# Float64 weights converted on four engines: Pool's integer sum moved from before the final merge to after it, in place on the weights

## The chip, the cores and the metric

The program runs on one core of one Trainium2 chip. A core has five engines, each with its own in-order queue of instructions: TensorE (PE, matrix products, with weight loads shown as PEld), VectorE (DVE), ScalarE (ACT), GpSimd (Pool) and SyncE (SP, which issues the transfers). [...]The metric is the device time of one execution in microseconds (us); lower is better.

## What is computed

The reference is a routed attention block followed by a feed-forward block:

```python
q_assign = argmax(q_n @ c_n.T);  k_assign = argmax(k_n @ c_n.T)        # 16 clusters per head
scores   = where(q_assign == k_assign, q @ k.T / sqrt(64), -1e9)       # batch 4, 8 heads, 768 tokens, 64 wide
attn_out = softmax(scores) @ v
x = attn_out as (3072, 512)
h = x @ w_in                                                          # w_in (512, 2048)
sp = log(1 + exp(h));  g = h * erf(sp)
out = (g @ w_out).astype(float32)                                     # w_out (2048, 512)
```

q, k, v and the centroids come as float32. The two weight matrices come as float64, so on the chip each value is two 32-bit words: a high word (sign, 11 bits of exponent, 20 of fraction) and a low word (the last 32 bits of the fraction). [...]the kernel makes float32 from the two words by integer operations.

## The kernel before

**Attention.** Heads go two at a time: 16 pairs (4 batches of 4 pairs), each with two halves of the queries (384 columns) and 6 blocks of 128 keys, which makes 12 units a pair. For a pair, `route` (line 276) transposes q and k on VectorE and finds clusters, and `shift` (line 352) computes bf16 products `sm` on TensorE, takes their row maxima `nmx` on VectorE, folds these into `nm`, transposes `nm` on TensorE (`pn`), copies it on ScalarE (`nmT`) and sends it by small transfers into a row of `qm`. For a unit, `scores` (line 409) makes `sc` on TensorE and exponentiates it into `pr` on ScalarE; `accumulate` (427) sums `pr` into `acc` on Pool; `attend` (440) multiplies `pr` by v into `av`. After 6 units `divide` (452) sums `acc` on TensorE (`psum`), makes its reciprocal with ScalarE's Ln and Exp (`inv`), refines it on VectorE (`den`) and writes the scaled `av` into `xT`.

**Feed-forward.** The 3072 tokens are 12 chunks of 256. `hidden` (line 519) multiplies `w_in` by `xT` into `hp`, which VectorE copies to `g`; `gate` (497) makes softplus and erf in two tiles `a_s` on ScalarE and multiplies them into `g` on Pool; `project` (543) multiplies `g` by `w_out` into `po`. These products are yielded one by one by `ffn_stream` (562) and fed between the attention units by `pump` (586). `sm`, `psum`, `pn`, `psim`, `hp`, `po` and `av` share one pool of four PSUM buffers, `sc` has two of its own. Softplus, erf, Ln and Exp lie in different function tables of ScalarE, and a table load goes in front of each that finds another table active.

**Conversion.** There are 32 steps (`w_steps`, line 172), each a block of 128 x 512 weights: 16 of `w_in`, then 16 of `w_out`. `fetch` (188) starts a step's transfer of 512 KB. The block lands in a quarter of the `w_out` tile that is not in use yet (places 0 to 3, so the trace calls these staging blocks `w_out`), or, for the late steps, in one of the two `a_s` tiles of the gate (place 4). The quarter also holds two scratch blocks: `m` for the rounding bits and `x` for the shifted value. One step is then

1. ScalarE: `x = |high word|` and `m` from the low word (`split`, 200);
2. VectorE: `x = max(x, tiny)`;
3. VectorE: `x = x << 3`, which puts exponent and fraction where float32 has them;
4. Pool: `x = x + m`, an integer sum that adds the three last bits, rounded, and mends the exponent's bias;
5. VectorE: `weights = (high word & sign bit) | x` (`join`, 207).

`convert` (215) is a generator with three yields a step. In its third part of step n it joins step n-1 (not n), starts a transfer, and splits step n+1. So the join of a step stands in VectorE's queue behind the maximum and shift of the next step. `converted` counts joined steps, and `hidden` and `project` yield nothing useful while a block that they need is not counted.

**Order.** `prepare(n)` (594) takes n parts of `convert`. Up to slot 44 of 48 (the first batch's units) the order in each queue is that of the program: the tuple `plan` (606) says for each of a pair's 12 slots how many parts of routing and of conversion go in front. From slot 45 (`FIRST`) on, `in_order` is off and a list scheduler with its own estimates places the instructions; `prepare(2)` is then called in each of five places per pair of units (line 702), except for some rest after a gate.

Of the kernel before, what the change touches and what calls it, by code (L numbers as in the profile page):

```python
# [8 lines left out]
F32 = mybir.dt.float32  # L9
BF16 = mybir.dt.bfloat16  # L10
U32 = mybir.dt.uint32
I32 = mybir.dt.int32
ALU = mybir.AluOpType
ACT = mybir.ActivationFunctionType
# [3 lines left out]
P = 128  # L18
# [48 lines left out]
def kernel(  # L67
# [13 lines left out]
    te, ve, ae, ge = (  # L81
        InOrder(tc, e, in_order) for e in (nc.tensor, nc.vector, nc.scalar, nc.gpsimd)
    )

    def pool(name, bufs, **kw):
        return ctx.enter_context(tc.tile_pool(name=name, bufs=bufs, **kw))

    const = pool("const", 1)
# [78 lines left out]

    two = const.tile([P, 1], F32, name="two")  # L170
    ve.memset(two, 2.0)
    w_steps = []
    for c in range(0, DFF, LC):
        for r in range(DM // P):
# [1 line left out]
    n_w_in = len(w_steps)  # L176
# [4 lines left out]
    converted = [0]  # L181

    def half_tile():
        return actp.tile([P, NFT // 2, TB], F32, name="a_s")

    steps = {}

    def fetch(done):

        for n in range(max(done + 1, 0), min(done + 5, len(w_steps))):  # L190
            at = places[n]
            if n in steps or (at < 4 and at in places[done + 1 : n]) or (at == 4 and n > done + 2):
                continue
            t = half_tile() if at == 4 else w_out[:, 4 * at : 4 * (at + 1)]
            t = t.rearrange("p f t -> p (f t)").bitcast(U32)
            nc.sync.dma_start(out=t[:, 0 : 2 * LC], in_=w_steps[n][1])
            raw = t[:, 0 : 2 * LC].rearrange("p (n w) -> p n w", w=2)
            steps[n] = raw[:, :, 1], raw[:, :, 0], t[:, 2 * LC : 3 * LC], t[:, 3 * LC : 4 * LC]

    def split(n):  # L200

        if n < len(w_steps):
            hi, lo, m, x = steps[n]
            ae.activation(out=x.bitcast(F32), in_=hi.bitcast(F32), func=ACT.Abs)
            ae.activation(out=m.bitcast(F32), in_=lo, func=ACT.Identity, bias=two, scale=2.0**-51)

    def join(n):
        hi, _, _, x = steps[n]
        ve.scalar_tensor_tensor(
            out=w_steps[n][0].bitcast(U32), in0=hi, scalar=0x80000000, in1=x,  # L210
            op0=ALU.bitwise_and, op1=ALU.bitwise_or,
        )
        converted[0] = n + 1

    def convert():

        split(0)
        for n in range(len(w_steps)):
            _, _, m, x = steps[n]
            xf, xi = x.bitcast(F32), x.bitcast(I32)  # L220
            ve.tensor_scalar(out=xf, in0=xf, scalar1=TINY_HI, scalar2=None, op0=ALU.max)
            yield
            ve.tensor_scalar(out=x, in0=x, scalar1=3, scalar2=None, op0=ALU.logical_shift_left)

            ge.tensor_tensor(out=xi, in0=xi, in1=m.bitcast(I32), op=ALU.add)
            yield
            if n > 0:
                join(n - 1)

                fetch(n - 2 if n < n_w_in else n - 1)  # L230
            split(n + 1)
            yield
        join(len(w_steps) - 1)

    load_qk(0)
    fetch(-1)
# [17 lines left out]
    for it in range(2):  # L254
# [4 lines left out]
            out=twice, in0=ss, scalar=inv, in1=norm, op0=ALU.mult, op1=ALU.add  # L259
# [3 lines left out]
            out=norm, in0=twice, scalar1=0.5, scalar2=(1e-6 if it else 0.0),  # L263
            op0=ALU.mult, op1=ALU.add,
# [325 lines left out]


    conv = convert()

    def prepare(n):
# [26 lines left out]
    for e in range(2):  # L621
        ve.tensor_copy(
            out=ccT[e * D : (e + 1) * D, :, e * C : (e + 1) * C],
            in_=pct[e * D : (e + 1) * D].rearrange("d (r e c) -> d r e c", e=2, c=C)[:, :, e],
# [10 lines left out]
    for e in range(2):  # L635
        ve.reduce_sum(
            out=own[:, e : e + 1],
            in_=ident.rearrange("p (g x c) -> p x g c", x=2, c=C)[:, e], axis=AX.XY,
# [106 lines left out]
```

## Time and profile before

The median is 1236.87 us over three runs (1235.66 to 1238.39). The profiled execution spans 1232.8 us.

| engine | busy us | share of the span |
|---|---|---|
| PE | 1162.9 | 94% |
| ACT | 568.8 | 46% |
| DVE | 534.6 | 43% |
| POOL | 464.9 | 38% |

The shares are averages over unlike stages. The first conversion instruction on ScalarE starts at 20.3 us and the last join ends at 285.6 us, so conversion touches only the first 290 us; the rest is attention and feed-forward products without a pause. In what follows, a line of the profile reads: source line (nearly always L58, the helper through which all operations are recorded, so that tiles tell them apart), engine, operation, tile written <- tiles read, shapes, count, then busy time, mean ns of one, and the idle time in front of them with what ended it. In a timeline the two first numbers are start and length in us.

The conversion's own instructions, from the groups of the trace by shape: ScalarE's absolute value takes 672 ns and its rounding 755 ns; VectorE's maximum and shift take 587 and 578 ns in the mean in the `w_out` places (median 427 for the two together), its join 866 to 958 ns in the mean (median 684 to 693); Pool's sum 1397 ns in the mean (median 1275).

### The profile page before, as it was taken

How to read it: one execution, taken by the hardware profiler on the slowest of the kernel's cores; microseconds unless marked ns; L12 is line 12 of the kernel's file. 1: busy time of each engine (PE TensorE's matmuls, PEld its weight loads, DVE VectorE, ACT ScalarE, POOL GpSimd, SP SyncE). 2: the span in 40 equal slices, each digit the busy share in tenths (PEclk: the TensorE clock that was granted, in tenths of full speed). 3: DMA queues.
4: the chain of work that ended last, by engine and by line, in shares of the span. 5: the costliest groups of instructions: out<-in, count | busy, mean ns of one | idle time of the engine just before them, and what ended most of it. 6: DMA issues, size and time to landing. Idle time of an engine off the chain costs nothing.

```text
span 1232.8 us, 13370 instructions
## 1 busy us (share of the span) xinstructions
PE 1162.9 (94%) x4897; PEld 622.3 (50%) x4897; DVE 534.6 (43%) x1000; ACT 568.8 (46%) x674; POOL 464.9 (38%) x462
## 2 busy tenths in 40 slices
PE   4788879988999998999999999999999999999998
PEld 1222236555454455555456455556456456576663
DVE  6888875564534344334344344333335112011121
ACT  3666646548352648165265445346264254032222
POOL 2567754345433344344143244225244343030200
PEclk7999889788999999999999999999999999999999
DMA  7334333131020202011020201002010000000000
GB/s 133 73 90 107 95 85 91 31 103 26 22 47 10 39 9 39 9 24 24 10 47 1 48 9 27 21 10 39 1 31 1 9 9 1 9 9 17 1 18 18
DMA packets 140753, 42.95 MB, mean 35 GB/s; under 512 B 133520, under 2 KB 133520, under 8 KB 140688
## 3 DMA queue, kind: packets, MB, share of 16 engines
q1 hardware_dynamic: 137552, 41.70, 15.2%
q10 hardware_dynamic: 3136, 0.39, 0.3%
q8 instruction: 39, 0.64, 0.2%
q14 instruction: 26, 0.21, 0.1%
HBM read 35.68 MB, written 6.29 MB: 34 GB/s over the span
## 4 chain that ended last, share of the span: by engine, by line
PE 69%; issue 6%; ACT 2%; DVE 2%; POOL 1%; DMA 1%; SPq 0%; ACTq 0%; DVEq 0%
PE po L58 25%; PE hp L58 23%; PE sc L58 10%; PE av L58 6%; PE sm L58 3%; PE psum L58 1%; ACT L58 1%; PE psim L58 1%; ACT inv L58 1%; DVE den L58 1%; POOL a_s L58 0%; DMA a_s<-in_moe_w_out_dram 0%; PE pn L58 0%; DVE w_out L58 0%; DVE xT L58 0%
## 5 line engine op out<-in xcount | busy, mean ns | idle before, releaser
L58 PE MATMUL hp<-xT,w_in 128*128 128x256 f32 x1536 | 387.4, 389 | 7.2 <-DVE xT L58 4.5
L58 PE MATMUL po<-w_out,g 128*128 128x512 f32 x768 | 367.8, 597 | 0.6 <-DVE den L58 0.6
L58 POOL TENSOR_TENSOR acc<-acc,pr 128x384 f32<-128x384 f32 x256 | 240.1, 968 | 321.7 <-ACT pr L58 321.6
L58 PEld LDWEIGHTS hp<-xT,w_in 128*128 128x128 f32 x1536 | 289.8, 193 | 125.1 <-issue 80.9
L58 DVE TENSOR_REDUCE nmx<-sm 128x1 f32<-128x384 f32 x384 | 195.2, 550 | 139.2 <-PE sm L58 138.3
L58 ACT ACT_TABLE_LOAD x112 | 143.7, 1283 | 235.9 <-DVE g L58 131.2
L58 ACT ACTIVATE pr<-sc 128x768 f32<-128x768 f32 x192 | 147.0, 806 | 156.8 <-PE sc L58 154.4
L58 PEld LDWEIGHTS po<-w_out,g 128*128 128x128 f32 x768 | 141.8, 190 | 106.1 <-issue 93.5
L58 PE MATMUL sc<-qT,kT 64*128 64x384 f32 x768 | 189.6, 543 | 4.5 <-ACT pr L58 4.4
L58 POOL TENSOR_TENSOR g<-a_s,g 128x512 f32<-128x512 f32 x88 | 111.1, 1296 | 209.3 <-ACT a_s L58 209.3
L58 DVE COPY g<-hp 128x512 f32<-128x512 f32 x96 | 65.9, 687 | 264.0 <-PE hp L58 263.8
L58 PE MATMUL av<-pr,in_v 128*64 128x386 f32 x768 | 142.9, 502 | 2.2 <-DVE nmx L58 2.2
L58 PE MATMUL sm<-km,qm 128*128 128x384 bf16 x384 | 104.3, 339 | 26.4 <-DVE nmx L58 14.6
L58 PEld LDWEIGHTS sc<-qT,kT 64*128 64x128 f32 x768 | 72.3, 193 | 88.6 <-issue 45.1
L58 POOL TENSOR_TENSOR acc<-pr,pr 128x384 f32<-128x384 f32 x64 | 64.9, 1034 | 102.0 <-ACT pr L58 102.0
L58 PEld LDWEIGHTS av<-pr,in_v 128*64 128x64 f32 x768 | 49.8, 138 | 89.9 <-issue 74.8
L58 PEld LDWEIGHTS <-qm 128*128 128x128 bf16 x384 | 35.1, 99 | 94.4 <-issue 71.8
L58 DVE SCALAR_TENSOR_TENSOR den<-psum,inv 128x384 f32<-128x384 f32 x32 | 17.8, 557 | 144.9 <-ACT inv L58 144.5
L58 PE MATMUL sc<-qm,km 64*128 64x384 bf16 x384 | 60.5, 330 | 2.1 <-DMA qm<-nmT 2.1
L58 ACT ACTIVATE a_s<-g 128x2048 f32<-128x2048 f32 x24 | 45.8, 1910 | 30.8 <-DVE g L58 30.7
L58 ACT ACTIVATE a_s<-a_s 128x2048 f32<-128x2048 f32 (+1 forms) x32 | 51.3, 1602 | 15.1 <-DMA a_s<-in_moe_w_out_dram 14.8
L58 ACT COPY nmT<-pn 6x128 bf16<-6x128 bf16 x32 | 8.0, 251 | 102.8 <-PE pn L58 102.2
(68 smaller groups left out, 609.8 us busy)
## 6 DMA issues: line engine op xcount, KB each, us to landing
w_out<-in_moe_w_in_dram SPq DMA_DIRECT2D x16, 512.0 KB, 4.7
in_q<-in_q_dram SPq DMA_DIRECT2D x64, 96.0 KB, 3.1
in_v<-in_v_dram SPq DMA_DIRECT2D x32, 192.0 KB, 3.0
out_dram<-osb SPq DMA_DIRECT2D x24, 256.0 KB, 2.0
in_k<-in_k_dram SPq DMA_DIRECT2D x60, 96.0 KB, 3.4
a_s<-in_moe_w_out_dram SPq DMA_DIRECT2D x8, 512.0 KB, 3.5
w_out<-in_moe_w_out_dram SPq DMA_DIRECT2D x8, 512.0 KB, 3.4
qm<-nmT SPq DMA_DIRECT2D x192, 0.2 KB, 1.7
```

Source lines behind the costliest of these rows:

```text
L58: ins = getattr(self.engine, name)(*args, **kw)
```

## The change

The conversion's last two operations change places. The shift gets a second operation, which masks the result to its lower 30 bits; the join follows on the same engine, takes the two upper bits of the high word instead of one, and writes the weights; and Pool adds the rounding bits last, in place on the weights. The bias of the exponent, which came in through the constant 2.0 in `m`, is now mended by the mask, so `m` becomes a plain rounded integer and the constant tile `two` goes. The three VectorE operations of a step no longer have Pool's sum between them, and a step is finished within its own turn: there is no join of an earlier step and no join after the loop. The call of `fetch` moves one part forward.

```diff
-    two = const.tile([P, 1], F32, name="two")
-    ve.memset(two, 2.0)
...
             ae.activation(out=x.bitcast(F32), in_=hi.bitcast(F32), func=ACT.Abs)
-            ae.activation(out=m.bitcast(F32), in_=lo, func=ACT.Identity, bias=two, scale=2.0**-51)
-
-    def join(n):
-        hi, _, _, x = steps[n]
-        ve.scalar_tensor_tensor(
-            out=w_steps[n][0].bitcast(U32), in0=hi, scalar=0x80000000, in1=x,
-            op0=ALU.bitwise_and, op1=ALU.bitwise_or,
-        )
-        converted[0] = n + 1
+            ae.activation(out=m.bitcast(I32), in_=lo, func=ACT.Copy, scale=2.0**-29)
...
         for n in range(len(w_steps)):
-            _, _, m, x = steps[n]
-            xf, xi = x.bitcast(F32), x.bitcast(I32)
+            hi, _, m, x = steps[n]
+            w = w_steps[n][0]
+            xf = x.bitcast(F32)
             ve.tensor_scalar(out=xf, in0=xf, scalar1=TINY_HI, scalar2=None, op0=ALU.max)
             yield
-            ve.tensor_scalar(out=x, in0=x, scalar1=3, scalar2=None, op0=ALU.logical_shift_left)
-
-            ge.tensor_tensor(out=xi, in0=xi, in1=m.bitcast(I32), op=ALU.add)
+            ve.tensor_scalar(
+                out=x, in0=x, scalar1=3, scalar2=0x3FFFFFFF,
+                op0=ALU.logical_shift_left, op1=ALU.bitwise_and,
+            )
+
+            fetch(n - 2 if n < n_w_in else n - 1)
             yield
-            if n > 0:
-                join(n - 1)
-
-                fetch(n - 2 if n < n_w_in else n - 1)
+            ve.scalar_tensor_tensor(
+                out=w.bitcast(U32), in0=hi, scalar=0xC0000000, in1=x,
+                op0=ALU.bitwise_and, op1=ALU.bitwise_or,
+            )
+
+            ge.tensor_tensor(out=w.bitcast(I32), in0=w.bitcast(I32), in1=m.bitcast(I32), op=ALU.add)
+            converted[0] = n + 1
             split(n + 1)
             yield
-        join(len(w_steps) - 1)
```

## The prediction, made before the result was known

> **What bounds the kernel now.** I read the page first (busy shares, then slices), then busy time by stretches, because an average can't say which stage the change touches.
>
> ```profile
> 20.00:140.00 120.00, 99.96 (x496) 31.50 (x495) 102.44 (x196) 74.04 (x115) 75.44 (x71) 0.92 0.35 83
> 140.00:200.00 60.00, 48.50 (x205) 23.83 (x205) 47.26 (x76) 28.90 (x45) 35.65 (x32) 0.86 0.35 90
> 200.00:300.00 100.00, 87.35 (x372) 54.05 (x370) 53.53 (x95) 62.27 (x70) 46.57 (x42) 0.86 0.27 62
> 300.00:1233.00 933.00, 920.85 (x3809) 510.91 (x3807) 320.40 (x582) 394.56 (x434) 300.54 (x296) 1.00 0.09 18
> ```
>
> Columns: stretch, its length, busy us of PE, PEld, DVE, ACT, POOL (with counts), PE's granted clock, the share of the DMA engines, GB/s. From 300 us on PE is busy 920.85 of 933 us at full clock. So the kernel is bound by PE, and every us that PE loses before 300 us arrives at the end, while what other engines gain is worth nothing unless PE waited for them. In the three stretches of conversion PE loses 20.0 + 11.5 + 12.7 = 44 us, and its clock is below 1. Until 140 us VectorE is busy 102.44 of 120 us and feeds PE late; afterwards it is not full, so what matters there is what its queue is blocked by. The waits of VectorE over the whole span:
>
> ```profile
> DVE w_out L58 <- POOL a_s L58: 9.2, 6, 3.2
> DVE w_out L58 <- POOL w_out L58: 5.0, 4, 1.5
> DVE w_in L58 <- POOL w_out L58: 1.7, 2, 1.4
> ```
>
> All three are a join that stands at the head of VectorE's queue until Pool's sum is done: 15.9 us, of which only 1.7 lie in the part ordered by the program. The timelines show what stands behind. VectorE, then PE:
>
> ```profile
> 161.87 0.42 DVE L58 TENSOR_SCALAR w_out<-w_out 128x512 uint32<-128x512 uint32 x1
> 163.66 1.47 DVE L58 SCALAR_TENSOR_TENSOR w_in<-w_out 128x512 uint32<-128x512 uint32 x1 [1.38 <-POOL w_out L58]
> 165.06 1.94 DVE L58 TENSOR_REDUCE nmx<-sm 128x1 f32<-128x384 f32 x4
> ...
> 175.32 1.74 DVE L58 SCALAR_TENSOR_TENSOR w_out<-w_out 128x512 uint32<-128x512 uint32 x1 [0.70 <-POOL w_out L58]
> 176.98 1.35 DVE L58 SCALAR_TENSOR_TENSOR den<-den,inv 128x384 f32<-128x384 f32 x1
> 178.25 1.35 DVE L58 SCALAR_TENSOR_TENSOR w_out<-w_out 128x512 uint32<-128x512 uint32 x1
> 179.53 0.74 DVE L58 SCALAR_TENSOR_TENSOR xT<-av,den 128x256 f32<-128x256 f32 x2
> ```
>
> ```profile
> 165.65 0.32 PE L58 MATMUL sm<-km,qm 128*128 128x384 bf16 x1 [2.32 <-DVE nmx L58]
> 168.18 0.27 PE L58 MATMUL pn<-identb,nm 128*6 128x128 bf16 x1 [1.41 <-DVE nm L58]
> 168.38 1.65 PE L58 MATMUL sc<-qT,kT 64*128 64x384 f32 x4
> 172.20 0.92 PE L58 MATMUL sc<-qT,kT 64*128 64x384 f32 x4
> 180.06 8.28 PE L58 MATMUL hp<-xT,w_in 128*128 128x256 f32 x26 [4.48 <-DVE xT L58]
> ```
>
> The join at 163.66 waits 1.38 us, and takes 1.47 instead of 0.68 since Pool's next sum has started; four row maxima stand behind it and PE loses 2.32. The same pattern delays `nm` (PE loses 1.41) and `xT` (4.48). Later, in the same PE timeline, PE waits 1.36 for `nmx` at 248.03, 3.50 for `nm` at 254.46, 1.95 for a `g` copy at 282.69 and 1.95 for `nm` at 285.77; in VectorE's queue the last three stand behind joins that waited 3.19, 1.98 and 0.51 us for Pool.
>
> **What the Trainium skill says.** "SBUF — State Buffer", section "Who interferes with whom": VectorE and GpSimd share a port pair as an exclusive lock, which a VectorE operation takes when it reads two SBUF inputs or runs in a two-port mode (the maximum and shift can, `nmx` from PSUM can't), and the second to come waits fully. The trace agrees: joins take 0.67 to 0.69 us free and up to 1.76 us, the row maxima 0.54 to 0.56 us under the same Pool load. "VectorE: DVE Perf Modes", section "The perf-mode tier table": `tensor_scalar` on fp32 in SBUF runs at two elements a cycle; the shift's free 0.42 us against the join's 0.68 fits. It names no other price for a second operation, and no row of this trace has one at this size. "TensorE: Matmul & The Clock Gate", Part 1: an idle PE falls back to a halved clock. The trace agrees: four `sc` products take 1.65 us just after those stalls and 0.92 later.
>
> **The change, part by part.** Per step there remain two ScalarE operations, three on VectorE and one sum on Pool, of the same sizes. The constant's memset (59 ns) goes; nobody waits for it.
>
> *ScalarE's rounding* loses its bias tile: between 0.67 us (the absolute value's row) and 0.755 us (today's), 32 x 0.08 = 2.7 us at most, hidden behind PE. I count 0. The order of the changed program, though, puts two more table loads into ScalarE's queue near the first gate (one more in the whole program): one exponential now stands between a softplus and an erf, and one absolute value between the next pair. A load is 1.283 us in the trace; at 240 us that delays the second erf and its successors by 1.28 + 0.67 = 1.95 us.
>
> *The shift's mask*: 0.42 us if the second operation is free; at one element a cycle about the join's 0.68, 32 x 0.26 = 8.3 us on VectorE. I take free.
>
> *Shift and join in sequence*: independent neighbours on VectorE overlap by about 0.09 us, dependent ones have a gap of 0.03 to 0.04, so some 0.12 us more, 16 x 0.12 = 1.9 us in the ordered part. About half of it meets PE: minus 1.0.
>
> *Join without Pool's wait, ordered part up to 180 us.* (a) Before `nm`: by the new order one join less lies between the shift at 161.87 and `nm`. From the shift's end, 162.29: four row maxima 1.94, a maximum 0.42 to 1.13, `nm` 0.16, so `nm` ends at 164.8 to 165.5 instead of 168.13. I take 2.9 us. (b) From `nm` to `xT` took 168.13 to 180.27 = 12.1 us, with ten conversion operations between; 5.7 us of it is waits and stretched lengths. In the new order six are left. The sum of free lengths is 2 x 0.68 + 4 x 0.42 + 0.54 + 0.56 + 0.74 = 4.9, but `den` needs `inv`, ready 4.8 us after `nm`, so at least 4.8 + 1.84 = 6.6; with up to 3 us of lock about 8. PE comes for `xT` 7.4 us after `nm`, so its wait falls from 4.48 to about 1: 3.5 us. (c) Clock: after the three stalls PE spends about 1.2 us too much at 168 to 171 and 8.28 - 26 x 0.224 = 2.5 at `hp` (0.224 is 7.17 us over the 32 at 192.56). Of 3.7 I take 1.5.
>
> *The moved operations* (three more after `xT`) land in 180 to 200 us, where VectorE waited for Pool 1.45 us three times: 0.
>
> *Last stage, 245 to 287 us.* Gone: the stalls at 282.69 and 285.77, up to 3.9 us, I take 2.0, since a `g` copy still stands behind conversions. Not gone: at 254.46 `nm` now stands behind the maximum of the next step, which needs a transfer into `a_s`; in the old trace its absolute value starts at 252.11, after a 4.67 us wait for that transfer, and the later erf pushes it. The maximum at 246.83 waited 2.19 us for ScalarE and is pushed too. Minus 2.0. Sum 0.
>
> *Pool's sum last*: the new wait is Pool's, for the join. Behind it in Pool's queue stand sums of `acc` and products of `g`, and behind those `psum` and `po`. It comes some 0.7 us later than before, but no longer against the join just issued (its mean 1.40 against 1.26 free), so Pool ends about 0.5 us later. `w_in` is used from 174 us, its first blocks being ready long before; the first `po` starts at 296 and the last join ended at 285.6. Hidden: 0.
>
> *fetch one part earlier*: a staging block is now freed by Pool's sum, which reads `m`, instead of by the join; both shifts are about a us and cancel: 0.
>
> Sum: 2.9 + 3.5 + 1.5 - 1.0 + 0 = 6.9 us. 1236.9 - 6.9 = 1230.0.
>
> **Rivals.**
>
> 1. *The wait changes its owner.* VectorE no longer waits for Pool but for transfers and ScalarE, and at 200 to 255 us the two table loads delay `pr` and `inv`. For it: the new order puts `nm` behind a maximum, and PE's 3.58 us wait for `den` at 217 is ScalarE's chain already. Against: the stalls at 165 to 180 depend on neither. Half the front gain, 3.5, minus 4 below and 1 for dependence: about 1238.
> 2. *The mask is not free* and the dependence is fully exposed. For it: VectorE is 85% busy until 140 us, with short PE waits for `nmx` throughout. Against: nothing in the trace has a slow one-input operation without Pool's hold. 16 x 0.26 = 4.2 plus 1.9, plus 4 of rival 1, minus 5 of gain: about 1242, slower.
> 3. *All stalls named go, with their clock*: 2.9 + 4.5 + 3.7 + 3.9 - 1 = 14: about 1223. Against it is the transfer above.
>
> **How the numbers follow.** The main case (1230, give or take 4) 0.52; rival 1 0.20; rival 2 0.13; rival 3 0.15. Bounds of 0.2% are 1234.4 and 1239.3. Faster: 0.52 + 0.15 + a quarter of rival 1 = 0.72; same: 0.14, nearly all from rival 1; slower: 0.14, rival 2 and a little. The range leaves out rival 2 and the far end of rival 3: 1221 to 1240.
>
> **What would show it.** Right: no VectorE wait for Pool's `w_in`, `w_out`, and PE's waits at 165, 168 and 180 together under 3.5 us instead of 8.2; the shift's free length still 0.42; PE's busy time after 300 us unchanged. Wrong: a shift of 0.65 us or more; more PE waits for `nmx` between 30 and 140 us; a VectorE wait for ScalarE in front of `nm` near 250 us above 5 us; `po` waiting for Pool.

## The result, and the profile after

The changed kernel takes 1223.06 us in the median (four executions, 1221.21 to 1229.21), the kernel before 1236.98 beside it: a ratio of 0.9896, with a 95% interval of 0.9858 to 0.9934. A second set of runs gave 1227.16 against 1237.75, ratio 0.9923 (0.9902 to 0.9944). So the gain is 11 to 14 us, where 6.9 were predicted.

The two profiles differ by less than that. The profiled execution of the changed kernel is the slowest of its four (1229.21, a span of 1227.4), that of the kernel before took 1234.62 (1232.8). The traces therefore show 5.4 us of the gain. They can be trusted for where things happen, and less for how much. Busy time by stretches, the changed kernel, with the columns of the prediction's first table:

```profile
20.00:140.00 120.00, 98.43 (x471) 30.64 (x472) 105.20 (x190) 70.47 (x111) 68.53 (x66) 0.88 0.37 86
140.00:200.00 60.00, 49.10 (x223) 21.79 (x220) 48.77 (x80) 31.26 (x49) 39.65 (x35) 0.93 0.32 86
200.00:300.00 100.00, 91.19 (x403) 56.15 (x402) 58.37 (x99) 70.35 (x77) 52.63 (x47) 0.93 0.25 62
300.00:1227.00 927.00, 913.35 (x3784) 507.69 (x3782) 318.16 (x580) 386.75 (x427) 298.24 (x294) 1.00 0.09 19
```

Until 140 us things are worse than before: PE is idle 21.6 us (20.0 before), its clock is 0.88 (0.92), VectorE is busy 105.20 us (102.44). From 140 to 300 us they are better: PE loses 10.9 + 8.8 us (11.5 + 12.7) and its clock is 0.93 in both stretches (0.86). From 330 us on every `nm` and `xT` of the changed kernel starts 5.4 us earlier than in the kernel before, without further change: everything happens ahead of that.

VectorE's waits over the whole span have no line for Pool any more; 15.9 us of them are gone. Of the conversion's waits these are left:

```profile
DVE a_s L58 <- ACT a_s L58: 6.8, 4, 3.1
DVE w_out L58 <- ACT w_out L58: 6.2, 5, 3.4
```

The first was 3.1 us before, the second 8.4. Now the timelines of the place that the prediction showed at 161 to 181 us. VectorE:

```profile
168.04 0.42 DVE L58 TENSOR_SCALAR w_out<-w_out 128x512 uint32<-128x512 uint32 x1
169.22 1.95 DVE L58 TENSOR_REDUCE nmx<-sm 128x1 f32<-128x384 f32 x4 [0.76 <-PE sm L58]
171.09 0.42 DVE L58 TENSOR_SCALAR w_out<-w_out 128x512 f32<-128x512 f32 x1
171.42 0.17 DVE L58 TENSOR_REDUCE nm<-nmx 128x6 bf16<-128x18 f32 x1
171.50 0.68 DVE L58 SCALAR_TENSOR_TENSOR w_in<-w_out 128x512 uint32<-128x512 uint32 x1
172.10 1.83 DVE L58 TENSOR_SCALAR w_out<-w_out 128x512 uint32<-128x512 uint32 x2
173.85 1.50 DVE L58 SCALAR_TENSOR_TENSOR w_in<-w_out 128x512 uint32<-128x512 uint32 x1
...
179.48 0.75 DVE L58 SCALAR_TENSOR_TENSOR xT<-av,den 128x256 f32<-128x256 f32 x2
```

PE:

```profile
166.78 0.32 PE L58 MATMUL sm<-km,qm 128*128 128x384 bf16 x1 [0.32 <-DVE nmx L58]
...
169.83 0.32 PE L58 MATMUL sm<-km,qm 128*128 128x384 bf16 x1 [0.32 <-DVE nmx L58]
...
171.64 0.22 PE L58 MATMUL pn<-identb,nm 128*6 128x128 bf16 x1 [0.69 <-DVE nm L58]
171.78 0.92 PE L58 MATMUL sc<-qT,kT 64*128 64x384 f32 x4
...
180.02 2.21 PE L58 MATMUL hp<-xT,w_in 128*128 128x256 f32 x9 [2.41 <-DVE xT L58]
```

No join stands between the shift (168.04) and `nm`: the row maxima follow at once, and the wait in front of them is for PE's own products. The three stalls of 2.32, 1.41 and 4.48 us have become 0.32 twice, 0.69 and 2.41. The four `sc` products after `nm` take 0.92 us, full clock, instead of 1.65. Yet `nm` itself starts at 171.42, later than the 167.97 of before, and `xT` at 179.48 where it was 179.53: the gain of this place only makes good what had been lost ahead of it.

To follow that I use two points: the `xT` at 156.05 us of the kernel before, where the ordered part nears its end, and the `nm` at 328.15, after the last conversion. Lateness is a kernel's start of the same instruction minus that of the kernel before. (It is the third pair's second half; one expectation calls it the fourth pair's.) The third number is the stretch: what VectorE's conversion operations ahead of the first point took beyond the free lengths of 0.685 us (join) and 0.42 us (maximum, shift), summed from the trace.

| kernel | median us | ratio | stretch | late at 156 | late at 328 |
|---|---|---|---|---|---|
| before | 1237 to 1239 | 1 | 6.0 | 0 | 0 |
| changed | 1223.06 | 0.9896 | 9.5 | +4.8 | -5.4 |
| changed, second run | 1227.16 | 0.9923 | 8.8 | +8.5 | -4.0 |
| late_join | 1230.59 | 0.9953 | 9.5 | +4.7 | -4.0 |
| join_own | 1248.38 | 1.0093 | 10.7 | +16.1 | +13.6 |
| old_first | 1218.73 | 0.9860 | 3.8 | -1.2 | -18.0 |
| old_first13 | 1222.61 | 0.9872 | 4.1 | -0.9 | -14.6 |
| old_first16 | 1222.34 | 0.9883 | 3.8 | -1.0 | -12.0 |
| new_first | 1241.63 | 1.0029 | 10.4 | +11.0 | +12.9 |
| no_sum | 1223.10 | 0.9878 | 11.9 | +7.7 | -10.3 |
| fetch_late | 1226.54 | 0.9908 | 8.8 | +7.7 | -7.3 |
| old_order | 1236.99 | 0.9993 | 6.7 | +2.8 | +3.6 |
| before_few_acc | 1224.93 | 0.9896 | 2.7 | -6.7 | -9.7 |
| free_ports | 1207.53 | 0.9752 | 1.2 | -8.2 | -29.2 |

The changed kernel loses about 5 to 8 us in the ordered part, and wins 10 to 13 behind it. About 1 us of each is only the marker's: four small products (two of `sm`, two of `sc` from `qm`; some 0.25 us each, an estimate from pairs of 0.33 and triples of 0.66 us) stand ahead of that `xT` in the changed kernel and behind it in the kernel before. Both halves needed a cause.

### The profile page after: what moved, and what is told of

It is laid out like the page before. It is cut to its first block, busy times and chain, and to the rows that moved or that the text cites. A ratio compares the mean times of both kernels' runs of the same rounds, so it can differ in the third digit from the quotient of the medians.

```text
span 1227.4 us, 13359 instructions
## 1 busy us (share of the span) xinstructions
PE 1158.3 (94%) x4897; PEld 618.2 (50%) x4897; DVE 541.5 (44%) x999; ACT 567.8 (46%) x675; POOL 465.8 (38%) x462
## 4 chain that ended last, share of the span: by engine, by line
PE 74%; DVE 11%; issue 7%; ACT 6%; DMA 2%; POOL 1%; SPq 0%; ACTq 0%; DVEq 0%
PE po L58 25%; PE hp L58 24%; PE sc L58 12%; PE av L58 7%; PE sm L58 4%; DVE nmx L58 3%; ACT L58 2%; DVE w_out L58 2%; DVE den L58 1%; DVE sims L58 1%; ACT inv L58 1%; PE psim L58 1%; PE psum L58 1%; ACT km L58 1%; ACT pr L58 1%
## 5 line engine op out<-in xcount | busy, mean ns | idle before, releaser
L58 DVE TENSOR_REDUCE nmx<-sm 128x1 f32<-128x384 f32 x384 | 195.4, 551 | 144.9 <-PE sm L58 144.0
L58 PE MATMUL sc<-qT,kT 64*128 64x384 f32 x768 | 185.3, 537 | 6.2 <-ACT pr L58 6.1
L58 PE MATMUL sm<-km,qm 128*128 128x384 bf16 x384 | 106.1, 342 | 31.3 <-DVE nmx L58 14.5
L58 ACT ACTIVATE a_s<-a_s 128x2048 f32<-128x2048 f32 (+2 forms) x40 | 55.8, 1413 | 13.3 <-DMA a_s<-in_moe_w_out_dram 8.9
```

What stands on the lines that cost most here:

```text
L58: ins = getattr(self.engine, name)(*args, **kw)
```

## Experiments

### The same kernel again

No edit; the question is how far the front's lateness repeats.

> The changed kernel once more, unedited, to see what of its trace repeats. If the lateness at the end of the ordered part (4.8 us against the kernel before at the xT of 156 us) belongs to the order of the instructions, it is there again, within 1 us, and the whole is 1221 to 1225. If it was TensorE's clock in that one execution, it is below 2 us.

Measured: 1227.16 us, above the 1221 to 1225, and a lateness at 156 us of +8.5 instead of +4.8: both are misses. The stretch repeated (8.8 against 9.5), and so did PE's idle time between the first `nm` and that `xT`: 21.5 and 21.7 us, where the kernel before has 18.9. What differs is PE's clock: in the same stretch the records show PE busy 115.3 us instead of 111.7 for the same products (109.6 in the kernel before), and after 80 us there are four stretches of 3.41 us at half clock instead of one. So one profile's lateness is uncertain by 3 to 4 us, and smaller differences are not read below.

### Which of the two moves: the sum's place or the join's turn

The change does two things to the order: Pool's sum goes behind the join, and the join goes into its own step's turn. Each alone makes a kernel. `late_join` has the sum last, but joins step n-1 in the turn of step n, as before:

```diff
+    def join(n):
+        ...    # join of two bits, then Pool's sum in place
-            ve.scalar_tensor_tensor(...)
+            if n > 0:
+                join(n - 1)
-            ge.tensor_tensor(out=w.bitcast(I32), in0=w.bitcast(I32), in1=m.bitcast(I32), op=ALU.add)
+                fetch(n - 2 if n < n_w_in else n - 1)
```

> The changed kernel with one thing put back: join and Pool's sum of step n-1 stand in the turn of step n, as the join of the kernel before did, and the transfer's call is at its old place. Pool's sum stays last. Theory of the wait: no VectorE wait for Pool, so the stretch after 160 us gains as in the changed kernel: 1221 to 1228. Theory of the place: as the kernel before, 1235 to 1239.

`join_own` is the kernel before with only the join's turn changed; Pool's sum stays ahead of it:

```diff
             if n > 0:
-                join(n - 1)
-
                 fetch(n - 2 if n < n_w_in else n - 1)
+            join(n)
```

> The kernel before with one thing changed: the join stands in its own step's turn, right behind the shift, but Pool's sum still comes between the two. Theory of the wait (the gain is that VectorE no longer stands waiting for Pool): each of 32 joins now waits 1.3 to 1.6 us for its own sum, some 45 us on VectorE, of which in the ordered part most reaches TensorE: 1250 to 1262. Theory of the place (the gain is that a step ends in its own turn, so that fewer conversion operations stand ahead of nm and xT): about as the changed kernel, 1221 to 1228.

Measured, in one set with the kernel before at 1237.75 us:

| | join a step later | join in its own turn |
|---|---|---|
| Pool's sum ahead of the join | 1237.75 (before) | 1248.38 |
| Pool's sum last | 1230.59 | 1227.16 (changed) |

The join's own turn by itself costs 10.6 us, since then each join meets the sum that it needs. VectorE's waits of `join_own`:

```profile
DVE w_in L58 <- POOL w_out L58: 12.9, 10, 1.5
DVE w_out L58 <- POOL a_s L58: 10.3, 7, 4.0
DVE w_out L58 <- POOL w_out L58: 3.8, 3, 1.5
```

27.0 us instead of 15.9, and now ten of them in the `w_in` steps, where VectorE is full. That is the theory of the wait, though the time falls just short of its 1250 to 1262, and 20 of 32 joins waited. Not all of it is waiting: up to the `xT` at 156 us VectorE waits 13.0 us for Pool instead of 0.3, its stretch is 4.7 us longer (10.7 against 6.0), and `join_own` is 16.1 late. The sum's place alone brings 7.2 us, and only with it does the join's own turn bring another 3.4. `late_join` came out between the two expected times, so neither theory had it right: the wait was gone entirely (no line for Pool), but the front was late by 4.7 us as in the changed kernel. That second fact matters. In `late_join` the maximum and shift of the next step lie between a step's shift and its join, so the dependence of neighbours, to which the prediction gave the front's loss, isn't there, and the loss is. One profile does not settle this, since most of these 4.7 us are longer busy time of PE (113.4 us against 109.6) and only 1.1 are idle time; `free_ports` below does.

One reservation goes with all these whole times. From slot 45 on the list scheduler orders each kernel anew, so a gain behind 156 us belongs to the move together with the order that came of it. PE's products stand in the same order in the kernel before and the changed one up to 217 us, and differ in places behind.

### One half of the change at a time

`old_first` keeps the old form for steps 0 to 13, most of `w_in` and nearly all of the ordered part, and uses the new one from step 14; `new_first` does the opposite.

```diff
+    def old(n):
+        return n < 14          # new_first: n >= 14
...
+            if n > 0 and old(n - 1):
+                join(n - 1)
+            if not old(n):
+                join(n)
```

> Steps 0 to 13 (the ordered part) converted as in the kernel before, steps 14 to 31 as in the changed kernel. If the ordered part loses 4 us because Pool's sum, released by the join, holds the ports against the next step's shift, and the free part gains about 10 us: the ordered part is level with the kernel before (within 1 us at the xT of 156 us) and the whole is 1217 to 1221, below both kernels. If the loss in front was chance: 1221 to 1225, and if the gain behind comes from the front's order: near 1237.

> The reverse of the mixed kernel: steps 0 to 13 as in the changed kernel, steps 14 to 31 as in the kernel before. If the two stages add up independently: late by 4 to 8.5 us at the xT of 156 us as the changed kernel is, and behind it VectorE waits for Pool again about 14 us as in the kernel before, so 1240 to 1246, slower than both. If the gain behind came from an earlier turn in front: 1230 or less.

Measured: 1218.73 us, ratio 0.9860 (0.9836 to 0.9885), and 1241.63, ratio 1.0029 (1.0020 to 1.0038). Both times lie in their ranges. The lateness at 156 us does not: -1.2 where 1 either way was expected, and +11.0 where 4 to 8.5 was, the latter in the slowest of `new_first`'s 22 executions (1247.49 us). The change makes the first 14 steps dearer by about 3 us (1241.63 against 1238.55), and from there on it wins 19.0 by the medians (1218.73 against 1237.75) and 17 by the ratio. The sum, -14 to -16, is somewhat more than the whole change's -11 to -14. `old_first` is better than both kernels. Busy time by stretches:

```profile
20.00:140.00 120.00, 100.64 (x495) 31.21 (x494) 99.81 (x196) 73.74 (x115) 74.11 (x69) 0.99 0.35 83
140.00:200.00 60.00, 50.28 (x226) 24.60 (x225) 52.20 (x82) 33.62 (x49) 37.76 (x34) 0.91 0.39 103
200.00:300.00 100.00, 91.25 (x426) 55.21 (x425) 57.38 (x100) 71.50 (x84) 54.24 (x48) 0.98 0.25 59
```

Until 140 us VectorE is busy 99.81 us instead of 105.20, and PE gets through 495 recorded products (496 before, 471 in the changed kernel).

Two more borders were tried. `old_first16` ends the old form after `w_in`'s 16 steps; in it the join of step 15 can read its staging block after a later step's transfer has come in, so one block of 128 x 512 weights may hold other values, while the work is the same. `old_first13` ends it after 13.

```diff
-        return n < 14
+        return n < 16          # old_first13: n < 13
```

> The mixed kernel with the switch two steps later: steps 0 to 15 as in the kernel before, only the 16 steps of w_out as in the changed kernel. Theory of the wait: two more joins wait for Pool, right in front of nm and xT at 160 to 180 us, where the kernel before lost most: 1220 to 1226, above the switch at 14. If the mixed kernel's gain belongs to its order by chance and not to the wait: no rule, anything from 1216 to 1236.

> As the run that keeps the old form in the first 14 steps, but the old form ends one step earlier (13 steps). In that run one join still waits 1.37 us for Pool at 162 us, and TensorE then loses 2.33 and 1.40 us at 164 and 167 us. If that wait is what costs there, the join now stands in its own turn without it, both stalls shrink to about 1 us together, and the time is 1214.5 to 1217.5 us. If the join only moves into the part before 156 us, where VectorE has no time to spare, the gain is given back: 1217.5 to 1221, no stall less or a later xT at 156 us (by 1 us or more).

Measured: 1222.34 (ratio 0.9851 to 0.9916) and 1222.61 (0.9845 to 0.9899). The first is inside its range. The second is a miss, and an instructive one. PE's stalls in `old_first13`:

```profile
163.35 0.32 PE L58 MATMUL sm<-km,qm 128*128 128x384 bf16 x1 [0.32 <-DVE nmx L58]
165.16 0.22 PE L58 MATMUL pn<-identb,nm 128*6 128x128 bf16 x1 [0.69 <-DVE nm L58]
175.40 2.82 PE L58 MATMUL hp<-xT,w_in 128*128 128x256 f32 x8 [4.27 <-DVE xT L58]
```

As the first theory had it, the two stalls of 2.33 and 1.40 us shrink to 0.32 and 0.69, and the `xT` at 156 us is no later than in `old_first` by more than 0.4 us. But PE then waits 4.27 us for `xT`, where `old_first` waits 1.4, and by 328 us the kernel is 3.5 us behind `old_first`. So the join's wait was the cause of those stalls, and taking it away was still not worth a gain: PE came sooner to the next thing it had to wait for. From the `xT` at 180 us to the `nm` at 226 us it takes 44.5 us where `old_first` takes 40.0, with 6.8 us of half clock against none (at most 3.4 us of products). In the profile 3.3 us more are lost after 440 us, where nothing of the conversion is left: most of it beside 3.4 us more of half clock near 450 us and 3.4 near 743. How much of this is the order, which also differs between the borders, and how much chance, stays open. All three are 14 to 19 us better than before (by ratio and by median); the choice among them is not explained.

### The arithmetic or the place

`old_order` has exactly the kernel before's order of operations and Pool's sum ahead of the join, but the changed arithmetic:

```diff
-            ae.activation(out=m.bitcast(F32), in_=lo, func=ACT.Identity, bias=two, scale=2.0**-51)
+            ae.activation(out=m.bitcast(I32), in_=lo, func=ACT.Copy, scale=2.0**-29)
...
-            ve.tensor_scalar(out=x, in0=x, scalar1=3, scalar2=None, op0=ALU.logical_shift_left)
+            ve.tensor_scalar(
+                out=x, in0=x, scalar1=3, scalar2=0x3FFFFFFF,
+                op0=ALU.logical_shift_left, op1=ALU.bitwise_and,
+            )
```

> The order of operations and Pool's place of the sum are those of the kernel before; only the arithmetic is the changed kernel's (shift with the mask as second operation, join with two bits, plain rounding without the bias tile). If the mask and the rounding cost nothing, and everything comes from the place of the sum: 1236 to 1240 us, the ratio within 0.2% of 1, and the fourth pair's xT (156 us) within 1.5 us of the kernel before. If the changed arithmetic is what makes the ordered part late: that xT is 4 us or more late, and without the gain of the back part the time is 1241 to 1246.

Measured: 1236.99 us against 1237.77, ratio 0.9993 (0.9983 to 1.0003). The mask, the two-bit join and the plain rounding together cost nothing that shows; everything comes from the order. The lateness at 156 us was +2.8 though, outside the 1.5 expected, with a stretch of 6.7 against 6.0 and some 7 us more of PE at half clock: the uncertainty of a single profile again.

### The transfer's place

```diff
-            fetch(n - 2 if n < n_w_in else n - 1)
             yield
             ...
             ge.tensor_tensor(out=w.bitcast(I32), in0=w.bitcast(I32), in1=m.bitcast(I32), op=ALU.add)
+            if n > 0:
+                fetch(n - 2 if n < n_w_in else n - 1)
```

> The changed kernel with the call of the transfer back in the third part of a step. My step counted the earlier call at 0: 1221 to 1229, as the changed kernel, and no wait of ScalarE for a transfer of weights longer by more than 3 us in all. If the earlier transfer carries a part of the gain: 1230 to 1234.

Measured: 1226.54 us, between the changed kernel's two results. Starting the transfer a part earlier is worth nothing that can be measured. The other half of the expectation is a miss: ScalarE waits 30.0 us for transfers of weights, 6.3 more than the changed kernel's 23.7, where at most 3 were expected. The time does not show it.

### Who holds VectorE in the ordered part

The stretch of the conversion operations rose with the sum last. By shapes, the ordered part (20 to 156 us), of the kernel before:

```profile
L58 DVE SCALAR_TENSOR_TENSOR w_in<-w_out 128x512 uint32<-128x512 uint32 x13 | 11.0, 849 | 0.3 <-POOL w_out L58 0.3
L58 DVE TENSOR_SCALAR w_out<-w_out 128x512 uint32<-128x512 uint32 x14 | 8.0, 573 | 0.2
L58 DVE TENSOR_SCALAR w_out<-w_out 128x512 f32<-128x512 f32 x15 | 7.5, 503 | 6.2 <-ACT w_out L58 6.2
```

and of the changed one:

```profile
L58 DVE TENSOR_SCALAR w_out<-w_out 128x512 uint32<-128x512 uint32 x14 | 10.6, 759 | 0.2
L58 DVE SCALAR_TENSOR_TENSOR w_in<-w_out 128x512 uint32<-128x512 uint32 x14 | 10.5, 751 | 0.3
L58 DVE TENSOR_SCALAR w_out<-w_out 128x512 f32<-128x512 f32 x15 | 8.9, 591 | 3.4 <-ACT w_out L58 3.4
```

The join got quicker (751 ns in the mean against 849), the shift slower (759 against 573), the maximum too. A timeline says why. VectorE and then Pool at one of the places, the kernel before:

```profile
91.36 0.87 DVE L58 TENSOR_SCALAR w_out<-w_out 128x512 f32<-128x512 f32 x2
92.15 0.69 DVE L58 SCALAR_TENSOR_TENSOR w_in<-w_out 128x512 uint32<-128x512 uint32 x1
```

```profile
92.38 1.58 POOL L58 TENSOR_TENSOR w_out<-w_out 128x512 int32<-128x512 int32 x1 [1.49 <-DVE w_out L58]
93.92 2.29 POOL L58 TENSOR_TENSOR acc<-pr,pr 128x384 f32<-128x384 f32 x2
```

and the changed kernel:

```profile
92.81 0.68 DVE L58 SCALAR_TENSOR_TENSOR w_in<-w_out 128x512 uint32<-128x512 uint32 x1
93.41 1.83 DVE L58 TENSOR_SCALAR w_out<-w_out 128x512 f32<-128x512 f32 x2
```

```profile
93.57 1.39 POOL L58 TENSOR_TENSOR w_in<-w_in,w_out 128x512 int32<-128x512 int32 x1 [4.16 <-DVE w_in L58]
```

A sum of Pool starts when the VectorE instruction that it needs has ended. At both places VectorE was in its next one by then, so what the sum can hold is the one after that. Before, the sum followed a shift; next on VectorE was the join, which had started 0.23 us sooner and held its ground, and Pool's sum waited (1.58 us instead of 1.26). Now it follows a join, and next are a maximum and a shift, together 1.83 us instead of 0.87. In the trace the maximum, which started 0.16 us ahead of the sum, takes its free 0.42 us; the shift behind it starts 0.29 us after the sum, ends 0.29 us after it, and takes 1.38. This is what the Trainium skill's page "SBUF — State Buffer", section "Who interferes with whom", calls an exclusive lock, which whoever starts first keeps for its whole instruction; the trace agrees on both sides, with the join that makes the sum wait and the shift that waits for it.

If the sum itself were all of it, taking it away would free VectorE:

```diff
-            ge.tensor_tensor(out=w.bitcast(I32), in0=w.bitcast(I32), in1=m.bitcast(I32), op=ALU.add)
```

> The changed kernel with Pool's sum left out: the weights lack their three last bits, rounded; all else, and the order on the other engines, is nearly that of the changed kernel. Theory of the lock (in the ordered part the sum, released by the join, holds the ports against the next step's shift, and pushes the sums of acc onto others): the ordered part loses nothing against the kernel before, between -2.5 and +1 us at the xT of 156 us, and the excess of the shifts there (5.8 us) falls to about 2. Rival, the dependence (shift and join now follow each other with a gap): the lateness stays at 4 us or more. Whole: 1214 to 1220 by the lock, 1223 to 1227 by the dependence.

Measured: 1223.10 us, the front 7.7 us late, the stretch 11.9 us: larger, not smaller. My first reading, that the sum's own holds are all of it, fell with this run: time and lateness are those expected of the rival, the dependence. By shapes, the same stretch of time:

```profile
L58 DVE SCALAR_TENSOR_TENSOR w_in<-w_out 128x512 uint32<-128x512 uint32 x14 | 14.3, 1019 | 0.3
L58 DVE TENSOR_SCALAR w_out<-w_out 128x512 f32<-128x512 f32 x15 | 9.4, 627 | 3.4 <-ACT w_out L58 3.4
L58 DVE TENSOR_SCALAR w_out<-w_out 128x512 uint32<-128x512 uint32 x14 | 9.2, 660 | 0.2
```

Now the joins are slow (1019 ns). The only large work left on Pool here are its sums of `pr` into `acc`. So the next question was whether those do it, in both kernels. They are left out beyond the first in four pairs, once in `no_sum` (`free_ports`) and once in the kernel before (`before_few_acc`):

```diff
-        if j > 0:
+        if j == 1 or (j > 1 and p >= HP):
             acc = st["acc", half]
```

> The changed kernel with almost all of Pool's sums in the ordered part left out: the conversion's sum in all steps, and in the first four pairs the sums of pr into acc beyond the first key pair of a half. If the late front is Pool's holds of the shared ports on VectorE's conversion operations, their stretch falls from 9.5 to under 2 us, and the xT at 156 us is no later than in the kernel before (-5 to +0.5 us); total 1212 to 1219. If the front is late for the order of VectorE's operations itself, the xT stays 4 us or more late and the total is 1220 to 1227.

> The kernel before, with the same sums of pr into acc left out in the first four pairs, and Pool's conversion sum kept. If in the kernel before the waiting conversion sum already keeps the sums of acc off the ports during maximum and shift, their removal gains little: stretch of the conversion operations 4 to 5.8 us (5.8 with them), xT at 156 us within 1.5 us, total 1234 to 1238. If the sums of acc hold VectorE in the kernel before as they do in the changed one, the stretch falls below 3 us and the xT comes 2 to 5 us earlier.

Measured: `free_ports` 1207.53 us, a stretch of 1.2 us, and 8.2 us earlier at 156 us than the kernel before. The stretch is as the ports would have it; the time and the `xT` are earlier still than their ranges. By shapes (20 to 150 us):

```profile
L58 DVE SCALAR_TENSOR_TENSOR w_in<-w_out 128x512 uint32<-128x512 uint32 x14 | 10.4, 742 | 0.3
L58 DVE TENSOR_SCALAR w_out<-w_out 128x512 uint32<-128x512 uint32 x14 | 6.3, 447 | 0.2
L58 DVE TENSOR_SCALAR w_out<-w_out 128x512 f32<-128x512 f32 x15 | 6.2, 411 | 5.1 <-ACT w_out L58 5.1
```

VectorE's order is that of the changed kernel, mask, dependence and all, and nothing is late. `before_few_acc` took 1224.93 us, with a stretch of 2.7 instead of 6.0 and the `xT` 6.7 us earlier. That is the fair comparison, with the same `acc` sums left out on both sides: -8.2 against -6.7. So the front's loss comes from Pool's sums, not from VectorE's own order. I had thought that in the kernel before the waiting conversion sum keeps the `acc` sums behind it off the ports. In that form the idea fell as well: the `acc` sums cost the kernel before 3.3 us of stretch. But they cost the order of the changed kernel 10.7 (11.9 without the conversion's sum, 1.2 without both). Leaving out `acc` sums also frees Pool and the chain behind `acc`, so the 8.2 and 6.7 us of earlier `xT` aren't all ports.

The traces can say whose holds these are. The table takes every VectorE operation between the first `nm` and the `xT` at 156 us, not the conversion's alone, and adds up what it took beyond its free length (taken as the length that only the quickest tenth of its kind in all these traces stays under), by the operation of Pool that ran beside it longest.

| kernel | beside the conversion's sum, us | beside `acc` sums, us |
|---|---|---|
| before | 1.5 | 13.2 |
| changed | 5.7 | 14.1 |
| changed, second run | 5.6 | 14.1 |
| late_join | 3.6 | 14.5 |
| no_sum | 0 | 18.3 |
| before_few_acc | 1.6 | 2.8 |
| free_ports | 0 | 1.7 |

With the sum last VectorE is held 5.1 us more, 4.2 of it beside the conversion's own sum. In the changed kernel this sum holds three shifts for about 1 us each, and `den` and `hot`, operations of the attention, for the rest. With that sum gone the `acc` sums hold VectorE nearly as much (18.3 us against 19.8 in all). So both are holders, and the one takes the other's place. What stays open is how much of the 5 to 8 us of lateness follows from this: PE's idle time rises by 2.6 to 2.8 us, and the rest is longer busy time of PE, which the added half-clock time there (4.6 and 14.6 us) can account for.

## Why the prediction was right or wrong

The direction was right, and 1223 to 1227 lies in the range, but at the low end: the total is that of rival 3, though not by rival 3's sum. By its steps:

**The wait.** Right. VectorE waits for Pool no more, and where the wait costs (join_own against the changed kernel) it is the main thing: 21 us between two kernels that differ in the sum's place, and otherwise in an arithmetic and a transfer's place that `old_order` and `fetch_late` show to be free.

**The mask and the rounding.** Right. The shift's free length is 0.41 to 0.43 us with two operations as with one, ScalarE's rounding fell from 755 to 666 ns, and `old_order` is within 0.2%. Rival 2's 8.3 us on VectorE do not exist.

**(a) and (b), the stage up to 180 us.** 6.4 us predicted; from `xT` at 156 to `xT` at 180 the kernel before took 23.5 us and the changed one 18.6, so 4.9. Its second half is exact: `nm` to `xT` went from 11.6 to 8.1 us. The first half is mis-sized: `nm` came 1.4 us nearer to the `xT` ahead of it, not 2.9. I had set VectorE's operations end to end from the shift on. With the join gone the row maxima wait for PE's `sm` instead (0.76 us at 169.22). PE's three waits add up to 3.7 us, where under 3.5 was to show the step right.

**"Pool's sum last ... Hidden: 0", and "shift and join in sequence", minus 1.0.** This is where the prediction failed. The ordered part lost 4.8 us in one profile and 8.5 in the other, and the cause was not the dependence (`free_ports` keeps it and is not late; `late_join` lacks it and is). I asked only who waits for Pool, and found nobody; I did not ask whom Pool's operation holds when it runs behind a different VectorE operation: 5.7 us of VectorE in the ordered part instead of 1.5. The prediction named the sign of it, more PE waits for `nmx` between 30 and 140 us, and in time it came: 9.3 us against 7.4, in ten waits instead of eleven. Two of these waits, in PE's timeline of the changed kernel, were 1.26 and 1.25 us before:

```profile
101.36 0.32 PE L58 MATMUL sm<-km,qm 128*128 128x384 bf16 x1 [2.34 <-DVE nmx L58]
...
137.85 0.32 PE L58 MATMUL sm<-km,qm 128*128 128x384 bf16 x1 [2.31 <-DVE nmx L58]
```

**(c), the clock.** Mis-sized: 1.5 us taken. From `xT` at 156 to `nm` at 328 PE was busy 150.5 us before and 144.0 after, 6.5 less, and its idle time fell by 3.6. Of the 10.3 us that the part behind 156 us won in this pair of profiles, 6.5 are thus less busy time, about 1 of it the four products that moved ahead. The half-clock time behind that point fell from 37.6 to 20.5 us, which is enough to explain the rest. An example is a stall on which I had put no price. PE's timeline before, with the stretch behind it:

```profile
216.99 0.48 PE L58 MATMUL sm<-km,qm 128*128 128x384 bf16 x1 [3.58 <-DVE den L58]
```

```profile
215.70:229.30 13.60, 12.31 (x29) 5.35 (x29) 8.86 (x18) 2.29 (x5) 4.55 (x4) 0.50 0.00 0
```

13.6 us at a clock of 0.50. In the changed kernel PE's order is another here (two `sc` products come first), the stall is 1.80 us, and the stretch half as long:

```profile
216.79 1.54 PE L58 MATMUL sc<-qT,kT 64*128 64x384 f32 x2 [1.80 <-ACT pr L58]
```

```profile
216.90:223.70 6.80, 6.80 (x18) 2.48 (x19) 3.84 (x7) 0.95 (x2) 2.79 (x3) 0.50 0.00 0
```

At half clock products take up to twice as long (four `sc` products 1.65 instead of 0.92 us in the prediction's timeline), so with a stall shorter by 1.78 us came up to 3.4 us more. The stall's length alone does not set it, though: at the same products `old_first` and `late_join` both wait 1.85 us for `den`, and the first has no half clock behind it, the second 10.24 us. The Trainium skill's "TensorE: Matmul & The Clock Gate", Part 1, which the prediction cited for the halved clock, stands; what I lacked was that what it takes here can exceed the stalls' own.

**Last stage, plus 2.0 minus 2.0.** The minus was wrong. The stall at 254.46 was "not gone" in the prediction; it went from 3.50 to 0.55 us:

```profile
251.99 0.22 PE L58 MATMUL pn<-identb,nm 128*6 128x128 bf16 x1 [0.55 <-DVE nm L58]
...
281.41 0.22 PE L58 MATMUL pn<-identb,nm 128*6 128x128 bf16 x1 [1.26 <-DVE nm L58]
```

`nm` does stand behind the maximum of the next step, as predicted, but that maximum waited only 1.09 us for ScalarE, in place of a join that waited 3.19 for Pool. Its absolute value began at 250.72 instead of 252.11 us; the likely reason is that the products of `g`, which free `a_s` for the transfer, began at 242.2 instead of 243.5. The two later stalls of 1.95 us became 0.73 and 1.26: 1.9 us gone where I took 2.0. One thing went the way the minus had it: the maximum that waited 2.19 us for ScalarE near 247 now waits 3.12, and PE loses 2.46 us at 246.87 for the `g` copy behind it, where it lost 1.36 for `nmx`. A wait of 1.72 us for `nmx` at 259.99 is new. In all PE waits 6.7 us in this stage instead of 8.8: 2.0 us won, where the sum had 0. The stage as a whole, from the `nm` at 226 to that at 286 us, is shorter by 4.5.

**The moved operations.** Counted as nothing, since VectorE had waited there for Pool. Wrong: from 180.81 to 188.97 us VectorE now runs nine conversion operations with one `g` copy among them, two pairs of them at 2.02 and 1.82 us, and the next `g` copy comes behind. PE's timeline has a stall there that the kernel before has not:

```profile
189.71 0.48 PE L58 MATMUL sm<-km,qm 128*128 128x384 bf16 x1 [2.37 <-DVE g L58]
```

The earlier transfer was rightly counted as nothing (`fetch_late`).

By stage, between the `xT` at 156 us, the `xT` at 180 and the `nm` at 226, 286 and 328 us:

| kernel | 156 to 180 | 180 to 226 | 226 to 286 | 286 to 328 |
|---|---|---|---|---|
| before | 23.5 | 46.4 | 59.6 | 42.6 |
| old_order | 24.0 | 46.5 | 59.8 | 42.7 |
| changed | 18.6 | 46.6 | 55.1 | 41.5 |
| changed, second run | 18.4 | 46.6 | 53.9 | 40.7 |

With the same order these repeat within 0.5 us, and the changed kernel's within 1.2. What it wins at 217 us it loses again in the same stage, at 189 us among other places.

So the sum was the net of two errors, and that the total lies in the range is partly luck. The front was taken at -1.0 and lost 5 to 8; the part behind it was taken at +7.9 and won 10 to 13 in the profiles. `old_first`, `old_first13` and `old_first16`, which keep the old front, win 14 to 19 in all. The gain was in the stalls and the clock of the part that was not full, and the cost in the part that was.

## What to carry to other kernels

When an operation of Pool moves to another place in the order, ask two things: who waits for it, and which VectorE operations start while it runs. Here the one right behind its releaser had already begun, and the next one was held. Ask also what Pool would run in its place: taking the sum away freed nothing. A move that pays where VectorE has slack can cost where VectorE is full; applied by stage (here the old form for 14 steps, the new one after), it gave 1218.73 us, better than either. A PE stall can bring half-clock time on top, and as two equal stalls of 1.85 us brought 0 and 10.24 us of it, one profile doesn't give its price.

## What was not expected of the hardware

- A `tensor_scalar` with two integer operations on 128 x 512 words took the 0.42 us of one with a single operation.
- How much the halved clock is worth in a kernel that PE bounds. It comes in multiples of 3.41 us (3.41, 6.83, 10.24, 13.65 and 20.48 us occur in these traces), which agrees with the windows of about 3.4 us in the Trainium skill's "TensorE: Matmul & The Clock Gate", Part 1; that the windows run freely, as it says there, would explain why executions differ, though no run here shows it. Before 340 us these stretches add up to 64.8 us in the kernel before, 51.2 in the changed one, 17.1 in `old_first` and 10.2 in `free_ports`. Executions with the same order differ in them, by 7 us between the kernel before and `old_order`, which goes far to explain why a single profile's lateness is uncertain.
- Removing an operation of Pool from the ports made VectorE's stretch larger (8.8 to 9.5 us, then 11.9), since Pool's other sums moved into its place: all the operations of VectorE together are held beside `acc` sums for 18.3 us instead of 14.1.
